# Kernel generation of a two-layer SSM and attention kernel: float32 identity matmuls for eight squarings and the coefficient sums

## Chip, cores, metric

The kernel runs on one core of one Trainium2 chip. The metric is device time in microseconds (us) of one execution, as the median of several runs. Engines are named as in the profile: PE (matrix engine; PEld its weight loads), DVE (vector engine), ACT (scalar engine), POOL (GpSimd), SP (the queue that issues nearly all DMAs).

## The reference

Four blocks work on x of shape 1 x 2048 x 512 in turn: dilated local attention (A), a state-space convolution (B), A, B. Both B blocks use the same parameters and so the same convolution kernel K, which depends on no activation:

```python
dt = jnp.exp(log_dt)[:, None]
logdA = dt * (A_re + 1j * A_im)
dB = dt * (B_re + 1j * B_im)
P = jnp.exp(logdA[:, :, None] * l[None, None, :])      # l = 0 .. 2047
K = jnp.einsum("dn,dnl,dn->dl", Cc, P, dB).real        # 512 x 2048
...
y = irfft(rfft(up) * rfft(Kp))[:L] + u * Dskip
x = x + A(layernorm(x)); x = x + B(layernorm(x)); x = x + A(layernorm(x)); x = x + B(layernorm(x))
```

Parameters and x are bfloat16.

## The kernel before

The program runs in stages: generation of K together with the start of the first attention layer (about 0 to 108 us), then the rest of attention, the convolution by a Fourier transform, and the two layers again. The change lies in the first stage, the function `k_gen`.

**How K is made.** With z = exp(dt * A), one complex number for each of 512 channels and 128 states, K at position l needs z to the power l. `k_gen` holds z as real and imaginary parts of 128 x 512 float32 (partition: state; free: channel) and squares it again and again: z, z^2, z^4, up to z^2048, eleven squarings k = 0 to 10. Before, one squaring was three instructions: `square(k)` on ACT squares both parts at once into `ws` (L1078), `double(k)` on DVE writes the imaginary part 2 * re * im (L1082), `differ(k)` on DVE writes the real part as the difference of the two squares (L1085). `power(k)` on ACT rounds each power to bfloat16 into one of two tables' seeds (L1096 into `Pw`, printed as `pow_t`, for k = 3 to 7; L1098 into `Bt`, printed as `B_t`, for the others), `power_neg(k)` stores the negated imaginary part (L1102 on ACT, L1104 on DVE).

**The coefficients.** `c_part` makes the complex product of B and dt * C: two float32 products into `t1` and `t2` (printed `t`), and their difference or sum into `c0` (printed `c_t`), all on DVE, all recorded at L1110, as `tt` is the helper there. Inputs arrive transposed by bfloat16 matmuls with `ident` or with the diagonal of dt (L1031) from `raw_*` tiles into PSUM tiles `pt`, a pool of four banks.

**The tables.** `bmul` fills `B_t` with products of powers (DVE, L1110; the temporary is `cm_t`). `table_head` (L1227) starts a chunk's table `A_t` with `c_t`; `levels` (DVE, L1110) doubles it five times with `pow_t`, two multiplies and an add per level. Four chunks of 32 channels use two buffers in turn. `product` (PE, L1268) multiplies `A_t` with `B_t` into `pk`, `produced` (ACT, L1276) copies that to `kgs`, from where DMAs store K.

**The other work of the stage.** Layer norm of x in four blocks: row sums on ACT (L1154, L145), means and variances on DVE (L1168, L1169, L1180), application on ACT and DVE (L195, L197), transposes on PE (L1196) and their evictions on ACT (L1199); projections on PE (L1206) and evictions on ACT (L1211). The stage ends with the first logits products `A_pr` on DVE (L342).

**The order.** Nothing is scheduled automatically here. `ORDERK` is a string that is walked letter by letter; each letter takes the next operation of one stream: s `square`, i `double` and `differ` in turn, b `power` and `power_neg`, C `c_part`, M `bmul`, T and U the levels of even and odd chunks, H a table head, l a, W, y, z, 3 the layer norm, t and e transposes and evictions, k q K Q projections and evictions, p and x products and evictions, c small DMAs, d loads of x, G and w constants and their store, o E copies within `kT_ext`, X the first logits products. Each engine runs its instructions strictly in the order in which the walk issued them, and waits on semaphores where it reads what another engine writes.

POOL makes constants in the first 15 us (`build_a_consts` and others): `ident`, `nident` (minus the identity), index tables and masks, all in bfloat16 or integers; `slot_mask` (L128) is the last of them.

Of the kernel before, what the change touches and what calls it, by code (L numbers as in the profile page):

```python
# [20 lines left out]
P = 128  # L21
# [13 lines left out]
N = 128  # L35
# [8 lines left out]
DQT = 8  # L44
NQT = DQG // DQT
ORDERK = """
isCbCiCbsiMaiCCbsiMiGGsbcCbMaTMiiMisMbiMbsGbMiGbiMTbcsibTTaiTcbTsbMTiiGbTGGsTMGciaiMTGMcabMGMaTM
asaMMGMlalTiWMlaaiyTbayiyTMawaMytatMTelkaeMsqMkdliqMaMKMaMMqMqWMlbQQMMMqMyHykUUakpKkyyttkaxUUpKU
kaUUUUaqUUxeUQppqHkdxxKUqeQTkTaUTklqT3paTqlKWTkQTplqkyqx3Ty3QKxT3TTpqlkTpyyHqWEUxktQlKtkUzkekeTK
zUUUkkzkUztKkKtkkTUpexUUKUEkUkeUkUKpKUokxkpxpKUkUxxkqUKEpxoqkkUpUUxopXXXKQpZxxZZ  # L50
"""
ORDER0 = """
KD KA KA KA KD KA KD KA KD KA KD kA KA kD KA KD UA KD UA UA UD KA kA kD kA UD
UA UD UA kD kA kD u UD u u UA m m m UA u u UD u UA m kD UA kD UA m
m u UA u m kA u kD u m kD u kD kA kA yA m YA m yD u yA u m m m
u u yA m m u YA m yA w000D yD yA YD yA w010D YA yD yA
"""
LATE0 = "a s t g r b m"
ORDERF = """
yA h00 YA h01 v100A v110D h10 a0 z12A p0 z11A n0D h11 w001A w011A S a1 p1 T0 E01A z13A E00D n1G H2  # L60
P02 a2 P00 Q00 p2 T1 E10D E11D P01 P11 P12 n2D H3 a3 P13 T2 P10 E20D E21D P03 p3 P21 P22 n3D
P23 T3 E30D E31A P20 x1
"""
ORDER1 = """
UA UD UA UD UA UA UD UA UD UD u u m m u u m m UA u UA UD m UA u u
UD UA u m m u u m m u YD m u YA YA m u yD m yA u u m m u w001A
m m yA yA w000D YA yD yA YD w011D yA yD w010D yA yD yA v101A v103D v113A v102D v112D v111D v110A v100A
"""

CORE0 = """  # L70
# [914 lines left out]
NIA = 32  # L985
CH = 32
NROW = 641


def k_gen(tc, nc, a_consts, ins, kd, la, x_v, lnst, zero, b_consts):  # L990

    B_L = (0, 1, 2, 3, 4, 5, 6, 7, 256, 258, 260, 262, 512, 516, 768, 772, 1024, 1280, 1536, 1792, 2048)
    NCH = P // CH
    with ExitStack() as ctx:
        pw = ctx.enter_context(tc.tile_pool(name="kg_pow", bufs=1))
        Bt = pw.tile([P, 2, P, NB, 4], BF16, name="B_t")
        Pw = pw.tile([P, NCH, 5, 4, 4 * CH], BF16, name="pow_t")
        c0 = pw.tile([P, 2, 4 * P], BF16, name="c_t")
        tab = [ctx.enter_context(tc.tile_pool(name="kg_tab0", bufs=1))]
        c_psum, c_small = ExitStack(), ExitStack()  # L1000
        sp = c_small.enter_context(tc.tile_pool(name="kg_small", bufs=1))
        pst = c_psum.enter_context(tc.tile_pool(name="kg_ps_t", bufs=4, space=PSUM))
        late = {}
        iotas, a_rest = a_consts(sp)
        ident = la.c["ident"]
# [13 lines left out]
        raw = {}  # L1019
        for name in ("A_im", "A_re", "B_re", "B_im", "C_re", "C_im"):  # L1020
            raw[name] = sp.tile([P, 4, N], BF16, name="raw_" + name)
            nc.sync.dma_start(raw[name][:], ins[name].rearrange("(t p) n -> p t n", p=P))
        x_load(0)
        zero()
        x_load(1)
# [22 lines left out]
        keyed()  # L1048
        steps, w2_store = rest()
        a_rest()  # L1050
        ws = sp.tile([P, 3, 4 * P], F32, name="ws")
        sn, cs = ws[:, 0], ws[:, 1]
        t1 = sp.tile([P, 4 * P], F32, name="t1")
        t2 = sp.tile([P, 4 * P], F32, name="t2")
        cur = {0: sp.tile([P, 2, 4 * P], F32, name="sq_z", tag="sq_z", bufs=2)}
        a_re, turn = cur[0][:, 0], ws[:, 2]
# [17 lines left out]
        nc.vector.tensor_tensor(cur[0][:, 1], a_re, sn, ALU.mult)  # L1074
        nc.vector.tensor_tensor(cur[0][:, 0], a_re, cs, ALU.mult)

        def square(k):
            nc.scalar.activation(ws[:, 0:2], cur[k][:], ACT.Square)  # L1078

        def double(k):  # L1080
            cur[k + 1] = sp.tile([P, 2, 4 * P], F32, name="sq_z", tag="sq_z", bufs=2)
            nc.vector.scalar_tensor_tensor(cur[k + 1][:, 1], cur[k][:, 0], 2.0, cur[k][:, 1], ALU.mult, ALU.mult)  # L1082

        def differ(k):
            nc.vector.tensor_tensor(cur[k + 1][:, 0], ws[:, 0], ws[:, 1], ALU.subtract)  # L1085

        def planes(k):
            return cur[k][:].rearrange("p r (c x) -> p r c x", c=NCH)

        def copy_by(eng):  # L1090
            return nc.scalar.copy if eng == "A" else nc.vector.tensor_copy

        def power(k):
            copy = copy_by(ENGK["b"][k + max(0, min(k - 3, 5))])
            if 3 <= k <= 7:
                copy(Pw[:, :, k - 3, 1::2, :].rearrange("p c r x -> p r c x"), planes(k))  # L1096
            else:
                copy(Bt[:, :, :, B_L.index(1 << k), :], cur[k][:].rearrange("p r (q g) -> p r q g", g=4))  # L1098

        def power_neg(k):  # L1100
            if ENGK["b"][2 * k - 2] == "A":
                nc.scalar.mul(Pw[:, :, k - 3, 2, :], planes(k)[:, 1], -1.0)  # L1102
            else:
                nc.vector.tensor_scalar(Pw[:, :, k - 3, 2, :], planes(k)[:, 1], -1.0, None, ALU.mult)  # L1104

        def power_copy(k):
            nc.sync.dma_start(Pw[:, :, k, 0, :], Pw[:, :, k, 1, :])
# [1 line left out]
        def tt(*args):  # L1109
            return lambda: nc.vector.tensor_tensor(*args)  # L1110

        def c_part():
            for q, (x0, y0, x1, y1, op) in enumerate((("C_re", "B_re", "C_im", "B_im", ALU.subtract),
                                                      ("C_re", "B_im", "C_im", "B_re", ALU.add))):
                yield tt(nat(t1[:]), T[x0], T[y0], ALU.mult)
                yield tt(nat(t2[:]), T[x1], T[y1], ALU.mult)
                yield tt(c0[:, q], t1[:], t2[:], op)

        def bmul(src, by, dst):
            s0, s1, st = src  # L1120
# [258 lines left out]
def kernel(  # L1379
# [200 lines left out]
```

## Time and profile before

| | us |
|---|---|
| median of 3 runs | 403.68 (402.94 to 405.08) |
| profiled execution, span from first to last instruction | 402.6 |
| DVE busy in the span | 383.5 |
| PE busy in the span | 328.0 |
| ACT busy in the span | 321.8 |
| POOL busy in the span | 59.1 |
| start of the first logits product on DVE (L342) | 103.41 |
| 11 squares on ACT (L1078), 128x1024 float32 | 1.05 each |
| 11 doublings (L1082) and 11 differences (L1085) on DVE | 0.68 each |
| 2 sums into c_t on DVE (L1110) | 0.73 each |

The profile is of one execution, so its span is compared with the runs' times only through the difference of 1.1 us to their median. The page gives busy time of each engine and, in 40 slices of 10 us, the busy share in tenths. In the order of time of an engine, each line has start, length, engine, source line, operation, written tile, read tiles, shape, and in square brackets how long the engine stood idle before it and who ended that. An instruction on DVE or ACT can start a little before the one ahead has ended, so the distance of starts is shorter than the length.

### The profile page before, as it was taken

What the parts mean: (1) busy time and instruction counts of PE and PEld (TensorE: products, weight loads), DVE (VectorE), ACT (ScalarE), POOL (GpSimd) and SP (SyncE); (2) the same over time, 40 slices, a digit from 0 to 9 for tenths busy, and PEclk for the clock granted to TensorE, in tenths of its full rate; (3) what the DMA queues carried; (4) which work ended last, traced back from release to release, by engine and by line L of the source; (5) the groups of instructions that cost most, each with busy time, mean ns of one, the idle gap of its engine ahead of it and who ended that gap; (6) DMA issues with size and microseconds to landing.
All of it is one profiled execution on the core that took longest, in us unless ns stands there. A gap on an engine that the chain in (4) does not pass through costs nothing.

```text
span 402.6 us, 14781 instructions
## 1 busy us (share of the span) xinstructions
PE 328.0 (81%) x6527; PEld 230.3 (57%) x6527; DVE 383.5 (95%) x460; ACT 321.8 (80%) x557; POOL 59.1 (15%) x75
## 2 busy tenths in 40 slices
PE   3000059999999989999998889999999998997895
PEld 2000026657735656756987888543456666566885
DVE  6999999999999999999999998979899999989994
ACT  7999888898656578988999987674666677989974
POOL 9402400000199500200600000100000001000000
PEclk9999997999999999999999999999999999999999
DMA  7952711115013875259236685730063019504606
GB/s 219 395 143 37 81 52 50 44 27 117 3 43 76 214 210 160 55 173 384 93 112 232 228 285 166 280 114 2 0 170 94 3 39 383 161 2 134 186 14 202
DMA packets 62323, 54.17 MB, mean 135 GB/s; under 512 B 33869, under 2 KB 50738, under 8 KB 60978
## 3 DMA queue, kind: packets, MB, share of 16 engines
q1 hardware_dynamic: 62250, 53.22, 43.5%
q8 instruction: 51, 0.84, 0.9%
q14 instruction: 14, 0.11, 0.1%
q10 hardware_dynamic: 8, 0.00, 0.0%
HBM read 30.15 MB, written 13.24 MB: 108 GB/s over the span
## 4 chain that ended last, share of the span: by engine, by line
PE 36%; DVE 31%; ACT 17%; issue 8%; DMA 5%; SPq 2%; POOL 1%; DVEq 0%; ACTq 0%; POOLq 0%
DVE pav L467 11%; PE pq L398 6%; PE pk L1268 5%; ACT a1s L791 5%; PE pp L1206 4%; DVE t L847 3%; PE pq L223 3%; DVE prod L342 3%; PE pp L282 3%; PE L L350 2%; ACT ub L860 2%; DVE B_t L1110 2%; DVE sq_z L1085 2%; DMA v_ext<-v_ext 2%; DMA kf_ring<-kf_dram 2%
## 5 line engine op out<-in xcount | busy, mean ns | idle before, releaser
L467 DVE TENSOR_TENSOR pav<-attn,v_ext 128x4096 bf16<-128x4096 bf16 (+1 forms) x34 | 72.4, 2168 | 0.4 <-DMA v_ext<-v_ext 0.3
L342 DVE TENSOR_TENSOR prod<-qT,kT_ext 128x4096 bf16<-128x4096 bf16 x29 | 67.0, 2341 | 1.4 <-PE L L350 0.9
L1196 PE MATMUL pt<-ident,x_blk 128*128 128x128 bf16 x64 | 5.9, 241 | 42.8 <-DVE x_blk L197 38.6
L1110 DVE TENSOR_TENSOR A_t<-A_t,pow_t 128x1024 bf16<-128x1024 bf16 (+4 forms) x46 | 38.3, 870 | 0.3
L492 PEld LDWEIGHTS <-pav 64*128 64x128 bf16 x1664 | 26.2, 95 | 13.5 <-DVE pav L467 8.6
L503 PE MATMUL pq<-wop,oT 128*128 128x512 bf16 x128 | 32.9, 379 | 0.7 <-ACT oT L494 0.7
L860 ACT CAST ub<-pb 128x1024 bf16<-128x1024 f32 x32 | 32.1, 1079 | 1.2 <-PE pb L809 1.2
L492 PE MATMUL po<-ident,pav 64*128 64x64 bf16 x1664 | 29.3, 190 | 4.2 <-DVE pav L467 3.2
L400 ACT CAST v_ext<-pq 128x512 bf16<-128x512 f32 x32 | 18.8, 586 | 16.2 <-PE pq L398 16.2
L809 PE MATMUL pb<-a1s,w_sb 128*128 128x64 bf16 x768 | 27.4, 193 | 5.0 <-ACT a1s L791 1.7
L398 PE MATMUL pq<-wv,xnT 128*128 128x512 bf16 x128 | 30.6, 380 | 0.0
L1206 PE MATMUL pp<-xnT,kT_ext 128*128 128x512 bf16 x96 | 27.1, 411 | 4.3 <-ACT kT_ext L1211 2.3
L1196 PEld LDWEIGHTS <-x_blk 128*128 128x128 bf16 x64 | 4.6, 107 | 44.8 <-DVE x_blk L197 38.8
L809 PEld LDWEIGHTS <-w_sb 128*128 128x128 bf16 x768 | 24.9, 98 | 7.2 <-issue 5.2
L791 ACT CAST a1s<-pb 128x1024 bf16<-128x1024 f32 x29 | 28.2, 1059 | 0.8 <-PE pb L802 0.8
L1268 PEld LDWEIGHTS <-A_t 128*64 128x64 bf16 (+1 forms) x512 | 22.9, 107 | 4.5 <-DVE B_t L1110 0.3
L1268 PE MATMUL pk<-B_t,A_t 128*64 128x84 bf16 (+1 forms) x512 | 24.6, 206 | 0.0
L791 DVE CAST a1s<-pb 128x1024 bf16<-128x1024 f32 x19 | 22.6, 1217 | 1.4 <-PE pb L802 1.3
L223 PE MATMUL pq<-xnT,kT_ext 128*128 128x512 bf16 x96 | 23.9, 380 | 0.0
L225 ACT CAST qT<-pq 128x512 bf16<-128x512 f32 x24 | 14.1, 586 | 9.3 <-PE pq L223 9.2
L509 ACT ACTIVATE x_sb<-pq 128x512 bf16<-128x512 f32 x24 | 14.3, 594 | 8.7 <-PE pq L503 8.7
L398 PEld LDWEIGHTS <-xnT 128*128 128x128 bf16 x128 | 11.6, 98 | 15.3 <-issue 3.0
(259 smaller groups left out, 897.0 us busy)
## 6 DMA issues: line engine op xcount, KB each, us to landing
w_sb<-w_dram SPq DMA_DIRECT2D x8, 1024.0 KB, 7.8
w_dram<-xnT SPq DMA_DIRECT2D x1, 4096.0 KB
kf_ring<-kf_dram SPq DMA_DIRECT2D x13, 256.0 KB, 4.8
kf_ring<-kf_dram SPq DMA_DIRECT2D x26, 128.0 KB, 4.3
v_ext<-v_ext SPq DMA_DIRECT2D x4, 784.0 KB, 6.6
x_blk<-in_A_x_dram SPq DMA_DIRECT2D x4, 512.0 KB, 4.1
kT_ext<-in_A_wqkv_dram SPq DMA_DIRECT2D x4, 512.0 KB, 9.2
x_sb<-in_A_x_dram SPq DMA_DIRECT2D x4, 512.0 KB, 5.3
```

Of the source, the lines that this page charges most:

```text
L223: nc.tensor.matmul(pq[:], lhsT=self.wqk[:, dt, ft * P:(ft + 1) * P], rhs=self.xnT[:, dt, q * 512:(q + 1) * 512], start=(dt == 0), stop=(dt ...
L342: nc.vector.tensor_tensor(pr, self.qT[q][:, ft].unsqueeze(1).to_broadcast([P, W, 4, P]), kap, ALU.mult)
L398: nc.tensor.matmul(pp[:], lhsT=xnT[:, dt, a * P:(a + 1) * P], rhs=wv[:, dt, :], start=(dt == 0), stop=(dt == NDT - 1))
L467: nc.vector.tensor_tensor(pv[:, i], attn[:, n % 4].unsqueeze(2).to_broadcast([P, W, DH // parts, H]), vap, ALU.mult)
L492: nc.tensor.matmul(po[:, h, 0, i * nt + ft, :], lhsT=pvf[rows, i, w, ft * P:(ft + 1) * P], rhs=ident[rows, rows], start=(w == 0 and ft + i ...
L503: nc.tensor.matmul(pw[:], lhsT=oT[:, ftp, :], rhs=self.wo[:, ftp, :], start=False, stop=(ftp == NDT - 1))
L791: (self.nc.scalar.copy if eng == "act" else self.nc.vector.tensor_copy)(dst, src)
L809: nc.tensor.matmul(p2[:, j, :], lhsT=self.w2[:, ec * EC + j, :], rhs=a1s[:, ec * EC + j, :], start=True, stop=True)
L860: nc.scalar.copy(ub[:], p2)
L1110: return lambda: nc.vector.tensor_tensor(*args)
L1206: nc.tensor.matmul(pps[kind, b, ft][:], lhsT=la.wqk[:, dt, c:c + P], rhs=la.xnT[:, dt, b * 512:(b + 1) * 512], start=(dt == 0), stop=(dt = ...
L1268: nc.tensor.matmul(o, lhsT=lhs, rhs=Bt[:, ri, c * CH + ql].rearrange("p b g -> p (b g)"), start=(not half and j % 4 == 0 and ri == 0), sto ...
```

## The change

The real part of a squaring is now made on PE for k = 3 to 10 (`SQ_PE = 3`): the identity times the first square plus the negated identity times the second, accumulated in one PSUM bank, in float32. The real part then stays in PSUM and is read there by `double`, `square` and `power`; the imaginary part has a tile of its own. Because the parts lie in different memories, `square` and `power` take two instructions of 512 where they took one of 1024. The two coefficient sums are made in the same way, with an ACT copy into `c_t`. POOL makes the float32 identities by two copies behind its other constants. Space comes from the raw tiles moving into the not yet used `qT` tiles and from a second pair of products placed in a not yet used part of `kT_ext`. `ORDERK` is another string of the same letters with the same counts. In the built program DVE has ten instructions fewer, ACT seventeen more (seven squares, eight power copies, two copies of sums), PE twenty float32 matmuls more, POOL two copies more; the number of DMAs is the same.

```diff
 ORDERK = """
-isCbCiCbsiMaiCCbsiMiGGsbcCbMaTMiiMisMbiMbsGbMiGbiMTbcsibTTaiTcbTsbMTiiGbTGGsTMGciaiMTGMcabMGMaTM
...
+isbCCiisisibsCCbCiiisCMMMbiTGsbbbMMMMMiiMMsbbiicTTTccasbGTTbTiiTTTcsiTTTGGiGGGbbbsGGMMMciiMaGMbaaa
...
+        ident32 = sp.tile([P, P], F32, name="ident32")
+        nident32 = sp.tile([P, P], F32, name="nident32")
+        nc.gpsimd.tensor_copy(ident32[:], ident[:])
+        nc.gpsimd.tensor_copy(nident32[:], la.c["nident"][:])
...
         def square(k):
-            nc.scalar.activation(ws[:, 0:2], cur[k][:], ACT.Square)
+            if k <= SQ_PE:
+                nc.scalar.activation(ws[:, 0:2], (im[k] or z0)[:], ACT.Square)
+                return
+            for r in range(2):
+                nc.scalar.activation(ws[:, r], cur[k][r], ACT.Square)
...
         def differ(k):
-            nc.vector.tensor_tensor(cur[k + 1][:, 0], ws[:, 0], ws[:, 1], ALU.subtract)
+            if k < SQ_PE:
+                cur[k + 1] = im[k + 1][:, 0], im[k + 1][:, 1]
+                nc.vector.tensor_tensor(cur[k + 1][0], ws[:, 0], ws[:, 1], ALU.subtract)
+                return
+            re = pst.tile([P, 4 * P], F32, name="pt")
+            nc.tensor.matmul(re[:], lhsT=ident32[:], rhs=ws[:, 0], start=True, stop=False)
+            nc.tensor.matmul(re[:], lhsT=nident32[:], rhs=ws[:, 1], start=False, stop=True)
+            cur[k + 1] = re[:], im[k + 1][:, 0]
...
+            for r, z in enumerate(cur[k]):
+                if 3 <= k <= 7:
+                    copy(Pw[:, :, k - 3, 1 + 2 * r, :], z.rearrange("p (c x) -> p c x", c=NCH))
+                else:
+                    copy(Bt[:, r, :, B_L.index(1 << k), :], z.rearrange("p (q g) -> p q g", g=4))
...
+        def c_sum(q, t):
+            pc = pst.tile([P, 4 * P], F32, name="pt")
+            nc.tensor.matmul(pc[:], lhsT=ident32[:], rhs=t[0], start=True, stop=False)
+            nc.tensor.matmul(pc[:], lhsT=(ident32 if q else nident32)[:], rhs=t[1], start=False, stop=True)
+            nc.scalar.copy(c0[:, q], pc[:])
+
+        prods = [(t1[:], t2[:]), [la.kT[:, 3, a:a + 8, :].rearrange("p a q -> p (a q)").bitcast(F32) for a in (14, 22)]]
...
-                yield tt(c0[:, q], t1[:], t2[:], op)
+                yield tt(nat(t[0]), T[x0], T[y0], ALU.mult)
+                yield tt(nat(t[1]), T[x1], T[y1], ALU.mult)
+                yield lambda: c_sum(q, t)
```

More of the change, by code (lines that the diff above doesn't have):

```diff
@@ L46 @@
 ORDERK = """
-isCbCiCbsiMaiCCbsiMiGGsbcCbMaTMiiMisMbiMbsGbMiGbiMTbcsibTTaiTcbTsbMTiiGbTGGsTMGciaiMTGMcabMGMaTM
-asaMMGMlalTiWMlaaiyTbayiyTMawaMytatMTelkaeMsqMkdliqMaMKMaMMqMqWMlbQQMMMqMyHykUUakpKkyyttkaxUUpKU
-kaUUUUaqUUxeUQppqHkdxxKUqeQTkTaUTklqT3paTqlKWTkQTplqkyqx3Ty3QKxT3TTpqlkTpyyHqWEUxktQlKtkUzkekeTK
-zUUUkkzkUztKkKtkkTUpexUUKUEkUkeUkUKpKUokxkpxpKUkUxxkqUKEpxoqkkUpUUxopXXXKQpZxxZZ
+isbCCiisibsCCbCiiisCMMMbiTGsbbbMMMMMiiMMsbbiicTTTccasbGTTbTiiTTTcsiTTTGGiGGGbbbsGGMMMciiMaGMbaaa
+aaisiMTMGMMlaaawMMlWMbaMsMMlMMiiyMTaaaMMMayylyaMlMbWMMMttHeeqlkkUUUUyqppyyyttUQUUdKqxxaaqakQpapk
+akkUKUUdkHUUxkUKKx3a3qTTUTqqeTTqppeQTTTTQx3TaaqqqqQpllQTWxqqlykk3QkkpTyTTKKyHUUkkUUkyKUUtxtkpeex
+lWkkUUKKlzzzEpkkzkkKxUUUUKttkUeUeUkpUKxkxkkkKKEEppUUooUUkkkkxxKKpoxXXqqQppXxxZZZ
 """
 ORDER0 = """
[L53 to L56, printed above, removed]
+KD KA KA KA KD KA KD KA KD KA KD kA KA kD KA KD UA KD UA UA UD KA kA kD kA UD UA UD UA kD kA kD u UD
+u u UA m m m UA u u UD u UA m kD UA kD UA m m u UA u m kA u kD u m kD u kD kA kA yA m YA m yD u yA u
+m m m u u yA m m u YA m yA w000D yD yA YD yA w010D YA yD yA
 """
@@ L60 @@
 yA h00 YA h01 v100A v110D h10 a0 z12A p0 z11A n0D h11 w001A w011A S a1 p1 T0 E01A z13A E00D n1G H2
-P02 a2 P00 Q00 p2 T1 E10D E11D P01 P11 P12 n2D H3 a3 P13 T2 P10 E20D E21D P03 p3 P21 P22 n3D
-P23 T3 E30D E31A P20 x1
+P02 a2 P00 Q00 p2 T1 E10D E11D P01 P11 P12 n2D H3 a3 P13 T2 P10 E20D E21D P03 p3 P21 P22 n3D P23 T3
+E30D E31A P20 x1
 """
 ORDER1 = """
-UA UD UA UD UA UA UD UA UD UD u u m m u u m m UA u UA UD m UA u u
-UD UA u m m u u m m u YD m u YA YA m u yD m yA u u m m u w001A
-m m yA yA w000D YA yD yA YD w011D yA yD w010D yA yD yA v101A v103D v113A v102D v112D v111D v110A v100A
+UA UD UA UD UA UA UD UA UD UD u u m m u u m m UA u UA UD m UA u u UD UA u m m u u m m u YD m u YA YA
+m u yD m yA u u m m u w001A m m yA yA w000D YA yD yA YD w011D yA yD w010D yA yD yA v101A v103D v113A
+v102D v112D v111D v110A v100A
 """
@@ L987 @@
 NROW = 641
+SQ_PE = 3
 def k_gen(tc, nc, a_consts, ins, kd, la, x_v, lnst, zero, b_consts):
@@ L1019, in k_gen @@
         raw = {}
+        q0, q1 = (la.qT[b][:].rearrange("p t a q -> p (t a q)") for b in range(2))
         for name in ("A_im", "A_re", "B_re", "B_im", "C_re", "C_im"):
-            raw[name] = sp.tile([P, 4, N], BF16, name="raw_" + name)
-            nc.sync.dma_start(raw[name][:], ins[name].rearrange("(t p) n -> p t n", p=P))
+            home = (q0, q1)[len(raw) // 4]
+            raw[name] = home[:, len(raw) % 4 * 512:(len(raw) % 4 + 1) * 512].rearrange("p (t n) -> p t n", n=N)
+            nc.sync.dma_start(raw[name], ins[name].rearrange("(t p) n -> p t n", p=P))
         x_load(0)
@@ L1054, in k_gen @@
         t2 = sp.tile([P, 4 * P], F32, name="t2")
-        cur = {0: sp.tile([P, 2, 4 * P], F32, name="sq_z", tag="sq_z", bufs=2)}
-        a_re, turn = cur[0][:, 0], ws[:, 2]
+        z0 = sp.tile([P, 2, 4 * P], F32, name="sq_z", tag="sq_zFalse", bufs=2)
+        cur = {0: (z0[:, 0], z0[:, 1])}
+        a_re, turn = cur[0][0], ws[:, 2]
         p_im = turned_by("A_im", by_dt)
@@ L1073, in k_gen @@
             T[name] = nat(b[:])
-        nc.vector.tensor_tensor(cur[0][:, 1], a_re, sn, ALU.mult)
-        nc.vector.tensor_tensor(cur[0][:, 0], a_re, cs, ALU.mult)
+        nc.vector.tensor_tensor(cur[0][1], a_re, sn, ALU.mult)
+        nc.vector.tensor_tensor(cur[0][0], a_re, cs, ALU.mult)
+        im = {0: None}
         def square(k):
-            nc.scalar.activation(ws[:, 0:2], cur[k][:], ACT.Square)
+            if k <= SQ_PE:
[3 more added lines that the diff above has]
+                nc.scalar.activation(ws[:, r], cur[k][r], ACT.Square)
         def double(k):
-            cur[k + 1] = sp.tile([P, 2, 4 * P], F32, name="sq_z", tag="sq_z", bufs=2)
-            nc.vector.scalar_tensor_tensor(cur[k + 1][:, 1], cur[k][:, 0], 2.0, cur[k][:, 1], ALU.mult, ALU.mult)
+            z = sp.tile([P, 1 if k >= SQ_PE else 2, 4 * P], F32, name="sq_z", tag=f"sq_z{k >= SQ_PE}", bufs=2)
+            nc.vector.scalar_tensor_tensor(z[:, 0 if k >= SQ_PE else 1], cur[k][0], 2.0, cur[k][1], ALU.mult, ALU.mult)
+            im[k + 1] = z
         def differ(k):
-            nc.vector.tensor_tensor(cur[k + 1][:, 0], ws[:, 0], ws[:, 1], ALU.subtract)
-        def planes(k):
-            return cur[k][:].rearrange("p r (c x) -> p r c x", c=NCH)
+            if k < SQ_PE:
[6 more added lines that the diff above has]
+            cur[k + 1] = re[:], im[k + 1][:, 0]
         def copy_by(eng):
@@ L1094, in power @@
             copy = copy_by(ENGK["b"][k + max(0, min(k - 3, 5))])
[L1095 to L1098, printed above, removed]
+            if k <= SQ_PE:
+                z = (im[k] or z0)[:]
+                if k >= 3:
+                    copy(Pw[:, :, k - 3, 1::2, :].rearrange("p c r x -> p r c x"), z.rearrange("p r (c x) -> p r c x", c=NCH))
+                else:
+                    copy(Bt[:, :, :, B_L.index(1 << k), :], z.rearrange("p r (q g) -> p r q g", g=4))
+                return
+            for r, z in enumerate(cur[k]):
+                if 3 <= k <= 7:
+                    copy(Pw[:, :, k - 3, 1 + 2 * r, :], z.rearrange("p (c x) -> p c x", c=NCH))
+                else:
+                    copy(Bt[:, r, :, B_L.index(1 << k), :], z.rearrange("p (q g) -> p q g", g=4))
         def power_neg(k):
             if ENGK["b"][2 * k - 2] == "A":
-                nc.scalar.mul(Pw[:, :, k - 3, 2, :], planes(k)[:, 1], -1.0)
+                nc.scalar.mul(Pw[:, :, k - 3, 2, :], cur[k][1].rearrange("p (c x) -> p c x", c=NCH), -1.0)
             else:
-                nc.vector.tensor_scalar(Pw[:, :, k - 3, 2, :], planes(k)[:, 1], -1.0, None, ALU.mult)
+                nc.vector.tensor_scalar(Pw[:, :, k - 3, 2, :], cur[k][1].rearrange("p (c x) -> p c x", c=NCH), -1.0, None, ALU.mult)
         def power_copy(k):
@@ L1110, in tt @@
             return lambda: nc.vector.tensor_tensor(*args)
-        def c_part():
[L1113 to L1116, printed above, removed]
-                yield tt(c0[:, q], t1[:], t2[:], op)
+        def c_sum(q, t):
[4 more added lines that the diff above has]
+        prods = [(t1[:], t2[:]), [la.kT[:, 3, a:a + 8, :].rearrange("p a q -> p (a q)").bitcast(F32) for a in (14, 22)]]
+        def c_part():
+            for q, (x0, y0, x1, y1) in enumerate((("C_re", "B_re", "C_im", "B_im"), ("C_re", "B_im", "C_im", "B_re"))):
+                t = prods[q]
+                yield tt(nat(t[0]), T[x0], T[y0], ALU.mult)
+                yield tt(nat(t[1]), T[x1], T[y1], ALU.mult)
+                yield lambda: c_sum(q, t)
         def bmul(src, by, dst):
```

## The prediction

> **What bounds the kernel now.** I read the page first (busy time, slices), then the table by stretches of time, then the order of time of each engine for the first 110 us, because the change touches kernel generation alone.
>
> ```profile
> PE 328.0 (81%) x6527; PEld 230.3 (57%) x6527; DVE 383.5 (95%) x460; ACT 321.8 (80%) x557; POOL 59.1 (15%) x75
> ...
> PE   3000059999999989999998889999999998997895
> ...
> DVE  6999999999999999999999998979899999989994
> ACT  7999888898656578988999987674666677989974
> ```
>
> ```profile
> 0.00:60.00 60.00, 9.75 (x53) 5.64 (x54) 55.97 (x100) 53.22 (x99) 20.22 (x46) 0.99 0.59 155
> 60.00:103.40 43.40, 41.27 (x540) 28.39 (x540) 42.13 (x68) 37.83 (x70) 0.00 (x0) 0.93 0.24 56
> ```
>
> The columns of the second fence are length, then PE, PEld, DVE, ACT and POOL busy, granted clock, DMA share, GB/s. In the first 60 us DVE is busy 55.97, ACT 53.22, PE 9.75: two full engines and an empty one. From 60 to 103.4 (where the first logits product starts on DVE) DVE and PE are both full. So time taken from DVE in the first 60 us is worth its full length if neither ACT nor a new wait takes it back; ACT has only 6.8 us of room.
>
> ```profile
> 11.00 0.68 DVE L1085 TENSOR_TENSOR sq_z<-ws 128x512 f32<-128x512 f32 x1
> 11.60 0.77 DVE L1110 TENSOR_TENSOR c_t<-t,t 128x512 bf16<-128x512 f32 x1
> 12.30 0.73 DVE L1082 SCALAR_TENSOR_TENSOR sq_z<-sq_z 128x512 f32<-128x512 f32 x1
> ...
> 17.36 0.69 DVE L1110 TENSOR_TENSOR c_t<-t,t 128x512 bf16<-128x512 f32 x1
> ...
> 18.30 0.23 DVE L1227 COPY A_t<-c_t 128x256 bf16<-128x256 bf16 x1
> ```
>
> The first two columns are start and length. A float32 row of 512 is listed with 0.68 us, but the next one starts 0.60 us later; I charge 0.60.
>
> **DVE's part.** Ten rows leave DVE: eight of the eleven L1085 subtractions (k = 3 to 10) and both c_t sums of L1110. 10 x 0.60 = 6.0 us. The doubling (L1082) stays and reads one operand in PSUM; the products at 9.81 do that and also stand 0.60 apart, so nothing is added.
>
> **The C sums, a new wait.** Each becomes two float32 matmuls and an ACT copy. The matmuls need the float32 identities, which POOL makes last.
>
> ```profile
> 9.31 1.11 POOL L114 TENSOR_SCALAR nident<-iota_id 128x128 bf16<-128x128 int32 x1
> ...
> 14.06 0.52 POOL L128 TENSOR_SCALAR slot_mask<-iota_slot_mask 4x16 bf16<-4x16 int32 x1
> ```
>
> POOL's list ends at 14.58; two 128x128 copies follow, each between 0.20 (the memset of that size at 1.03) and 1.11 (nident). With 0.5 the first sum cannot start before 15.1, although its products are ready at 11.1. No float32 matmul is in the trace. Below, one cannot be cheaper than one bf16 matmul of 512 columns; its price depends on the clock:
>
> ```profile
> 54.41 0.15 PEld L1206 LDWEIGHTS <-kT_ext 128*128 128x128 bf16 x1 [0.28 <-issue]
> 54.83 0.15 PEld L1206 LDWEIGHTS <-kT_ext 128*128 128x128 bf16 x1 [0.28 <-issue]
> ...
> 116.54 2.76 PE L398 MATMUL pq<-wv,xnT 128*128 128x512 bf16 x12
> 119.14 0.59 PE L425 MATMUL L<-mx,nident 128*128 128x512 bf16 x2
> ```
>
> After a pause the matmuls between these weight loads follow each other at 0.43 us; in the steady stretch it is (119.14 - 116.54) / 12 = 0.22. Above, a product of two float32 numbers cut into three bf16 parts each would be nine such passes. DVE's rows charge a float32 operand twice a bf16 one (0.60 for 512 against 0.60 for 1024 at 41.43), so I take two parts per operand, 2 x 2 = 4 passes: 1.72 us at half clock, 0.87 at full. [...]
>
> PE has been idle since 8.4, so the first sum runs at half clock: 15.1 + 2 x 1.72 + 0.2 of drain = 18.7. Its copy (L1141) stands on ACT behind the square of k = 2 and ahead of the B_t copy of k = 2, the square of k = 3 and the second copy, so ACT stands still from 14.6 to 18.7, then does copy 0.5, B_t copy 0.95 and square 0.95 to 21.1; the second sum is ready about 21.2 (half of it at full clock), copied by 21.8. DVE's table head (18.30 above) reads both and stands in the new order after one doubling more and two sums less: due at 18.2, it waits 3.6 us, with all of DVE's queue behind it. The ends: 0.9 with one pass, 9 with nine. A wait of 0.5 for the square of k = 1 is added at 12.3, where the c_t sum used to stand.
>
> **The squarings.** One round from k = 3 on: square of the real part 0.6 (512 on ACT), two matmuls 1.73 at full clock, drain and handovers 0.3: 2.6 us. In the trace the squares of k = 4 to 8 start at 20.87, 23.28, 27.26, 30.29 and 33.64, 3.2 apart, so at full clock the rounds lie beside DVE's other work and cost nothing. Uncovered, at half clock, a round is 0.6 + 3.44 + 0.3 = 4.3, 1.1 late each, and DVE's next doubling with all behind it waits. Which clock?
>
> ```profile
> 52.44:55.85 3.41, 3.16 (x15) 1.00 0.40 107
> 55.85:59.26 3.41, 1.40 (x8) 1.00 0.12 47
> 59.26:62.68 3.42, 2.29 (x7) 0.50 0.00 0
> 219.69:223.10 3.41, 2.22 (x66) 1.00 0.81 299
> ```
>
> Columns: length, PE busy, clock. A stretch with 3.16 of 3.41 busy was followed by full clock, one with 1.40 by half, 2.29 did not lift it again; 2.22 at 219.69 did not drop it. The sums and the first squaring keep PE full from 15.1 to about 22, so it goes to full clock there; then 1.73 of every 2.8 to 3.0 is 60%, which kept it. The last two or three squarings lie 5 to 7 us apart (25 to 35% busy) and fall back to half. [...]
>
> **ACT.** Seven squares and eight power copies become two halves (2 x 0.50 for 0.95, +0.05 to 0.1 each, 15 times: 1.0), two C copies add 1.0. With the standstill (4.1, and 0.1 before the second copy) ACT is 6.2 later, less some 3.8 us of idle time it has from 25 to 60: about 2.4 late at 60. Its rows there feed the transposes and B_t. PE waited 3.1 us between 56.6 and 61 for ACT's evictions in the old order, so nothing covers it in PE. The late half-clock squarings lie here too. Ends 0 and 2.8; I take 1.4.
>
> **Order written anew.** The table's rows now stand as multiply, multiply, add directly behind one another. A dependent neighbour costs 0.11 more (27.87 to 28.18 is 0.31, an independent one 0.20); about nine more of them up to the first logits: 1.0. Moved DMAs: the same 251 on SP's queue in nearly the same order; the raw loads get another home (qT, first written at 60.34), and so does the second pair of products (columns of kT_ext, first written at 57.98), both long after their last reader. POOL's two copies are followed by nothing before 38. After 60 us the order of the chunks is shuffled with the same rows; nothing is charged, with 1 us either way.
>
> **Sum:** -6.0 + 0.5 + 3.6 + 1.4 + 1.0 = +0.5 us. Profiled span 402.6 becomes 403.1; the runs shown have a median 1.1 above that span (403.68), so 404.2. What this kernel can tell from no change is about 0.5%, 2.0 us.
>
> **Rivals.**
>
> 1. *Cheap float32 matmuls, faster.* With two passes (0.86 at half clock) the first sum is out at 17.0, the second copy done at 19.8: DVE waits 1.6; rounds are 1.8, late ones harmless, ACT 0.5 late. -6.0 + 0.5 + 1.6 + 0.5 + 0 to 0.5 = -3.4 to -2.9: 400.5. For it: only one operand carries more than bf16 (the identity is 0, 1, -1). Against it: the identity was widened to float32, so the operation is float32 in both.
>
> 2. *PE stays at half clock through the squarings, slower.* Place: the doublings of k = 4 to 8. Each round 4.3 for 3.2, five rounds late by 1.1 = 5.5, stall at the table head 4.2. -6.0 + 0.5 + 4.2 + 5.5 + 1.4 + 1.0 = +6.6: 410.3. It decides once a round exceeds the 2.8 to 3.2 us that DVE's rows give it, that is once a float32 matmul takes more than some 1.1 us. For it: 2.29 of 3.41 busy did not lift the clock at 59.26, and rounds are lighter than that. Also for it: a weight load of its own in each pass (0.1, the page's PEld L1196 has a mean of 107 ns) left uncovered would bring 0.87 to 1.27. Against it: PE is solidly busy from 15.1 to 22. If it were both, or nine passes, the eighth squaring would reach past 55 and push the transposes behind it on PE; that goes beyond 415.
>
> 3. *The saving arrives whole.* If the sums hid wholly (identities early, full clock) -6.0 + 0.5 + 1.0 + 0 = -4.5: 399.2. POOL's end at 14.58 speaks against it.
>
> **How the numbers follow.** The even case has 0.47 (own range 401.5 to 407), rival 1 with rival 3 0.25, rival 2 with its worse forms 0.28. Of the even case 0.03 lies below 401.7 and 0.07 above 405.7. So faster 0.28, same 0.37, slower 0.35. The range takes in rival 1 and most of rival 2: 400.2 to 411.
>
> **What would show it.** Right: ACT idle some 4 us before the first c_t copy, released by PE; DVE idle 3 to 4 us before COPY A_t<-c_t; float32 rows of about 1.7 us at 15 us and 0.9 later; DVE ten rows fewer; the first logits product (L342 at 103.41) within 2 us of where it was. Wrong: rows of about 0.5 (rival 1), or sq_z doublings waiting on PE 1 us each from 25 to 45 (rival 2). A granted clock other than half at 15 us would undo the stall's size.

## The result and the profile after

The changed kernel takes 405.04 us (median of 20 runs, 404.1 to 407.14), the kernel before 404.06 (20 runs beside them). The ratio is 1.0026, interval 1.0015 to 1.0038: 1.0 us slower, which is clear of the noise but within the bound of 0.5% that the prediction takes as no change, and 0.8 us from the 404.2 predicted. The profiled span is 403.9 (402.6 before).

From the page of the changed kernel, and from its table by stretches (length, then PE, PEld, DVE, ACT, POOL busy, clock, DMA share, GB/s):

```profile
PE 345.7 (86%) x6519; PEld 238.4 (59%) x6567; DVE 378.1 (94%) x450; ACT 324.1 (80%) x574; POOL 54.2 (13%) x77
```

```profile
0.00:60.00 60.00, 29.82 (x81) 12.57 (x82) 53.01 (x94) 53.20 (x111) 15.46 (x48) 0.88 0.57 148
60.00:103.40 43.40, 41.84 (x541) 29.23 (x550) 40.10 (x65) 39.79 (x76) 0.00 (x0) 0.93 0.27 66
```

DVE has ten instructions and 5.4 us of work less. PE has 17.7 us more. ACT is as full in the first 60 us as it was (53.20; 53.22 before). In order of time, the places that the prediction named, on POOL, PE and ACT:

```profile
13.66 0.28 POOL L1055 CAST ident<-ident 128x128 f32<-128x128 bf16 x1
13.90 0.28 POOL L1056 CAST nident<-nident 128x128 f32<-128x128 bf16 x1
```

```profile
13.99 2.07 PE L1139 MATMUL pt<-t,ident 128*128 128x512 f32 x2 [5.77 <-POOL ident L1055]
15.86 1.91 PE L1140 MATMUL pt<-t,nident 128*128 128x512 f32 x2
17.57 1.32 PE L1139 MATMUL pt<-kT_ext,ident 128*128 128x512 f32 x2
18.73 1.02 PE L1140 MATMUL pt<-kT_ext,ident 128*128 128x512 f32 x2
20.34 1.13 PE L1103 MATMUL pt<-ws,ident 128*128 128x512 f32 x2 [0.60 <-ACT ws L1087]
...
44.91 2.08 PE L1103 MATMUL pt<-ws,ident 128*128 128x512 f32 x2 [6.00 <-ACT ws L1090]
```

```profile
17.81 0.59 ACT L1141 CAST c_t<-pt 128x512 bf16<-128x512 f32 x1 [3.15 <-PE pt L1140]
```

The first sum waits for POOL; from the start of its second matmul to the next sum is 17.57 - 15.86 = 1.71 us at half clock, and 0.97 at full between the two matmuls of a squaring (21.31 after 20.34). That the clock is half at 14 us is read from these lengths; the profile's clock column doesn't show it, as it reads 1.00 from 14.75 to 18.17. ACT stands still 3.15 us. DVE, four of its places:

```profile
20.80 0.25 DVE L1260 COPY A_t<-c_t 128x256 bf16<-128x256 bf16 x1 [2.44 <-ACT c_t L1141]
...
72.87 1.29 DVE L137 BATCH_NORM_STATS2 ln_bn<-x_blk 128x6 f32<-128x512 bf16 x2 [2.46 <-DMA x_blk<-in_A_x_dram]
...
103.36 6.69 DVE L341 TENSOR_TENSOR A_pr<-qT,kT_ext 128x4096 bf16<-128x4096 bf16 x3
...
116.08 1.23 DVE L413 TENSOR_REDUCE mx<-L 128x128 bf16<-128x1024 f32 x1 [1.25 <-PE L L324]
```

The table head waits 2.44. At 60.28 DVE starts the table of chunk 1, 2.7 us ahead of the kernel before (62.97). At 72.87 it has waited 2.46 for a load. The first logits product stands at 103.36 (103.41 before). The row `mx` at 116.08 is DVE's first maximum over the logits and is taken as the end of the stage from here on; it has waited 1.25 for PE, where the kernel before started it with no wait:

```profile
115.59 1.21 DVE L414 TENSOR_REDUCE mx<-L 128x128 bf16<-128x1024 f32 x1
```

So 0.5 of the 1.3 us by which the profiled spans differ lie in the stage, and 0.8 behind it. There PE stands still once near the end, and the trace shows nothing that released it:

```profile
394.59 0.19 PE L877 MATMUL pb<-WpJ,t 64*128 64x64 bf16 x1 [0.81 <-issue]
```

The profiles of e1 and e2 have it at the same row (0.76 and 0.52), that of the kernel before doesn't. It is most likely the greater part of the 0.8; its cause is open.

What PE did up to the end of the stage, first the kernel before, then the changed one (first projection and last table products):

```profile
53.60 2.98 PE L1206 MATMUL pp<-xnT,kT_ext 128*128 128x512 bf16 x8 [0.25 <-ACT xnT L1199]
...
104.89 4.34 PE L1268 MATMUL pk<-B_t,A_t 128*128 128x84 bf16 x96
```

```profile
60.40 0.59 PE L1239 MATMUL pp<-xnT,kT_ext 128*128 128x512 bf16 x1 [1.80 <-ACT xnT L1232]
...
107.20 2.91 PE L1301 MATMUL pk<-B_t,A_t 128*128 128x84 bf16 x64
```

PE starts its projections 6.8 us later and ends its table products at 110.1 instead of 109.2, almost without a pause in between. So three theories for why a lighter DVE brought nothing: LOAD (the wait at 72.87 took the lead back), HEAD (the late identities cost ACT, DVE and then PE), PE (PE's full stretch from 60 to 110 sets the end, and starts late).

### The profile page after: what moved, and what is told of

It is laid out like the page before. It is cut to its first block, busy times and chain, and to the rows that moved or that the text cites. A ratio compares the mean times of both kernels' runs of the same rounds, so it can differ in the third digit from the quotient of the medians.

```text
span 403.9 us, 14829 instructions
## 1 busy us (share of the span) xinstructions
PE 345.7 (86%) x6519; PEld 238.4 (59%) x6567; DVE 378.1 (94%) x450; ACT 324.1 (80%) x574; POOL 54.2 (13%) x77
## 3 DMA queue, kind: packets, MB, share of 16 engines
q1 hardware_dynamic: 62250, 53.22, 43.0%
## 4 chain that ended last, share of the span: by engine, by line
PE 37%; DVE 26%; ACT 18%; issue 6%; SPq 5%; DMA 4%; POOL 3%; DVEq 0%; ACTq 0%; POOLq 0%
DVE pav L466 7%; PE pq L397 6%; DVE A_t L1135 4%; PE pq L222 3%; PE pk L1301 3%; DVE t L846 3%; PE pp L281 3%; SPq L1406 3%; PE pp L1239 2%; PE pb L808 2%; ACT ln_junk L144 2%; PE L L349 2%; ACT ub L859 2%; ACT a1s L790 2%; DVE prod L341 2%
## 5 line engine op out<-in xcount | busy, mean ns | idle before, releaser
L502 PE MATMUL pq<-wop,oT 128*128 128x512 bf16 x123 | 31.9, 379 | 3.8 <-issue 2.5
L1239 PE MATMUL pp<-xnT,kT_ext 128*128 128x512 bf16 x87 | 23.8, 400 | 3.0 <-ACT xnT L1232 1.8
L1103 PE MATMUL pt<-ws,ident 128*128 128x512 f32 x16 | 10.2, 720 | 16.1 <-ACT ws L1090 15.5
L502 PEld LDWEIGHTS <-oT 128*128 128x128 bf16 x128 | 12.4, 98 | 13.4 <-ACT oT L493 1.3
```

Of the source, the lines that this page charges most:

```text
L502: nc.tensor.matmul(pw[:], lhsT=oT[:, ftp, :], rhs=self.wo[:, ftp, :], start=False, stop=(ftp == NDT - 1))
L1239: nc.tensor.matmul(pps[kind, b, ft][:], lhsT=la.wqk[:, dt, c:c + P], rhs=la.xnT[:, dt, b * 512:(b + 1) * 512], start=(dt == 0), stop=(dt = ...
```

## The experiments

All in one table, with 12 runs for each experiment (4 for e7 and e8). Ratio is to the kernel before on the same chip (403.85 to 404.18 in these comparisons). The last three columns are from the profiled execution: start of PE's first projection, end of its last table product, start of DVE's first `mx` (L413/L414), the end of the stage.

| run | median | ratio (interval) | first proj. | last product | mx |
|---|---|---|---|---|---|
| before | 404.06 | 1 | 53.60 | 109.23 | 115.59 |
| changed | 405.04 | 1.0026 (1.0015-1.0038) | 60.40 | 110.11 | 116.08 |
| e1 fill the DVE wait | 405.37 | 1.0030 (1.0006-1.0053) | 61.63 | 111.21 | 117.21 |
| e2 identities early | 402.06 | 0.9961 (0.9939-0.9983) | 57.97 | 106.94 | 112.93 |
| e3 fewer projections, changed | 402.92 | 0.9978 (0.9960-0.9996) | 60.40 | 108.57 | 114.55 |
| e4 fewer projections, before | 406.07 | 1.0040 (1.0019-1.0061) | 53.59 | 108.00 | 114.51 |
| e5 identities early, PE kept busy | 401.02 | 0.9921 (0.9894-0.9948) | 58.33 | 105.47 | 111.45 |
| e6 sums on DVE | 404.24 | 1.0016 (0.9988-1.0044) | 62.62 | 112.22 | 118.20 |
| e7 new code, old order | 415.80 | 1.0260 (1.0214-1.0306) | 66.38 | 120.18 | 127.29 |
| e8 old code, new order | 412.37 | 1.0204 (1.0165-1.0242) | 68.45 | 117.65 | 123.63 |
| e9 sums on DVE, PE warmed first | 403.67 | 1.0003 (0.9980-1.0026) | 59.63 | 108.34 | 114.31 |
| e10 changed, PE kept busy | 402.98 | 0.9979 (0.9961-0.9996) | 60.41 | 107.55 | 113.52 |
| e11 before, PE kept busy | 405.13 | 1.0031 (1.0015-1.0047) | 55.43 | 109.06 | 115.42 |
| e12 before, matmuls far ahead | 404.72 | 1.0017 (0.9998-1.0036) | 53.58 | 109.47 | 115.83 |

**e1: fill the wait for the load.** In `ORDERK`, one level step (U) of chunk 1 is taken ahead of the two statistics (3):

```diff
-akkUKUUdkHUUxkUKKx3a3qTTUTqqe...
+akkUKUUdkHUUxkUKKxU3a3qTTTqqe...
```

> The changed kernel with one multiply of the table's last level of chunk 1 (a DVE row of 2.29 us) moved ahead of the two row statistics of block 3, so that it lies in the 2.46 us that DVE waits for the load of block 3 at 70.4. Theory LOAD (that wait took back what DVE had gained): the first logits product comes from 103.36 to about 101.1 and the time falls by 2.3 us, to 402.7. Theory PE (PE is full from 60 to 110 and its last table product at 110.1 decides when DVE may go on at 116): the last product stays within 0.6 us, DVE's wait of 1.25 us at 116 grows by what DVE gains, the time stays within 0.6 us of 405.0.

DVE's order of time in e1:

```profile
69.22 4.49 DVE L1135 TENSOR_TENSOR A_t<-A_t,pow_t 128x4096 bf16<-128x4096 bf16 x2
73.93 1.29 DVE L137 BATCH_NORM_STATS2 ln_bn<-x_blk 128x6 f32<-128x512 bf16 x2 [0.21 <-DMA x_blk<-in_A_x_dram]
...
82.29 0.16 DVE L1201 SCALAR_TENSOR_TENSOR ln_msq<-ln_s 128x4 f32<-128x4 f32 x1 [1.01 <-ACT ln_junk L1187]
83.04 0.16 DVE L1202 SCALAR_TENSOR_TENSOR ln_veps<-ln_s,ln_msq 128x4 f32<-128x4 f32 x1 [0.59 <-ACT ln_junk L144]
```

The wait for the load went from 2.46 to 0.21, and nothing was gained: 1.0 and 0.6 us came back as waits for ACT's row sums, and the wait at `mx` grew from 1.25 to 1.55. From PE's first projection to its last table product it took 49.6 us here and 49.7 in the changed kernel. This profile has a handicap, as PE's first projection came 1.2 us late in it (see the last section); but the median of twelve runs shows no gain either, where LOAD asked for 2.3. LOAD falls; the stage follows PE. The wait for the load is itself PE's lateness: the queue that issues this load waits for PE's transposes,

```profile
SPq L1015 <- PE pt L1229: 15.1, 2, 9.7
```

(the changed kernel; us in total, times, longest), and where PE's transposes came earlier with DVE's order untouched (e5 and e10 below), DVE had no wait there.

**e2: the identities early.** POOL makes them behind the memset of `B_t`; the two copies at L1055 go.

```diff
+        ident32 = sp.tile([P, P], F32, name="ident32")
+        nident32 = sp.tile([P, P], F32, name="nident32")
+        nc.gpsimd.tensor_copy(ident32[:], ident[:])
+        nc.gpsimd.tensor_scalar(nident32[:], ident32[:], -1.0, None, ALU.mult)
         pdt = pst.tile([P, 4, P], F32, name="pt")
```

> The changed kernel with the two float32 identities made on POOL at about 4.8 us, ahead of its index tables and masks. Theory HEAD (the C sums wait for POOL from 11.1 to 14.0; ACT stands still 3.15 us there and DVE 2.44 at the table head; ACT is full until 60, so its delay goes on to the layer norm and to PE's first projection at 60.4): first sum at 11.2, ACT's 3.15 us and DVE's 2.44 us gone or under 0.6, first squaring on PE at about 17.5, first projection at about 57.5, last table product at about 107, time 2.5 to 3.3 us less, 402. Theory PE alone (PE's stretch starts late for another reason): DVE gains 2.4 us and gives them back at 70 and 116, time 404.5 to 405. Theory LOAD alone: DVE's wait at 70 grows from 2.46 to nearly 5 us, time 404 to 405.

PE and DVE of e2:

```profile
10.61 2.05 PE L1139 MATMUL pt<-t,ident 128*128 128x512 f32 x2 [3.19 <-POOL off_WpJ L662]
...
57.97 0.59 PE L1239 MATMUL pp<-xnT,kT_ext 128*128 128x512 bf16 x1 [1.80 <-ACT xnT L1232]
```

```profile
18.18 0.23 DVE L1260 COPY A_t<-c_t 128x256 bf16<-128x256 bf16 x1
```

The waits of 3.15 on ACT and 2.44 on DVE are gone, PE's first projection comes 2.4 us earlier, its last table product 3.2, and the time falls by 3.0 to 402.06, as HEAD said.

**e3 and e4: less work for PE.** In `proj`, in the changed kernel and in the one before:

```diff
-            for dt in range(2 * h, 2 * h + 2):
+            for dt in range(2 * h, 2 * h + 2) if kind == "k" else (3 * h,):
```

> The changed kernel without half of the contraction of the query projections (16 of 32 matmuls of 512 columns; the queries come out wrong). PE has 3.5 us less to do at full clock. Theory PE: the last table product comes 1.5 to 3 us earlier, DVE's wait of 1.25 us at 116 goes, time 1.3 to 3 us less, 402 to 403.7. Theory LOAD: only the two to four of these matmuls that stand ahead of the transposes at 67.6 count, the load comes 0.4 to 0.9 us earlier, time 0.4 to 0.9 us less.

> The kernel before without half of the contraction of the query projections (16 of 32 matmuls; the queries come out wrong). If DVE alone bounds the kernel before, as the prediction took it: no difference, within 0.4 us of 404.1, although PE has 3.5 us less to do. If PE bounds the stage there too: 1 us less or more.

In the changed kernel 3.5 us less work on PE bring 2.1 us: its last table product comes 1.5 earlier, the wait at `mx` is 0.47. PE holds. The rest of the 3.5 is not gained, since PE now waits 1.9 us for ACT's evictions of the queries. In the kernel before the stage also ends 1.1 us earlier, so DVE was not its only bound; yet the time is 2 us longer. In the profile 2.7 us are lost behind the stage. A standstill of PE at L492, for which the profile gives no releaser, is 1.0 us here and 0.3 in the kernel before. Why is open (e12).

**e5, e10, e11: PE kept busy.** Matmuls whose results nobody reads, in e5 and e10 (8 before the last squaring, 3 behind each of the first four transposes, 9 behind the block's last), in e11 with 15 between the projections instead of the first 8:

```diff
+            for _ in range(WARM.get(k, 0)):
+                nc.tensor.matmul(re[:], lhsT=ident[:], rhs=la.wqk[:, 0, 0:512], start=True, stop=True)
...
+                    n = WARM_T[a] if (b, d, di) == (0, 0, 0) else WARM_P if (b, d, di, a) == (0, 1, 1, 3) else 0
+                    if n:
+                        wu = pst.tile([P, 4 * P], F32, name="pt")
+                    for _ in range(n):
+                        nc.tensor.matmul(wu[:], lhsT=ident[:], rhs=la.wqk[:, 0, 0:512], start=True, stop=True)
```

> The kernel with early identities (402.1) and, beside it, 29 more bfloat16 matmuls on PE whose results nobody reads: 8 before the last squaring, 3 behind each of the first four transposes, 9 behind the last transpose of block 0. They are to keep PE busy from about 46 to 58, so that the projections from 58 on and the first table products run at full clock (in the early-identity profile the clock is half until 61.9). Theory CLOCK (PE sets the end of the stage, and its first 4 us there run at half clock): the six or seven projections from 58 take 1.5 us instead of 3.2, the last table product comes from 106.9 to about 105, time 1 to 2 us less, 400.1 to 401.1. Rivals: ACT's evictions, not PE, set the pace up to 65, then the time stays at 402 within 0.5; or the added matmuls stand in the way of transposes at half clock, then 1 us more.

> The changed kernel, its identities late as they are, with the 29 matmuls that nobody reads around the transposes of block 0 (as in the early-identity kernel that had them). Theory CLOCK: the first projections from 60.4 and table products from 63.8 at full clock, the last table product from 110.1 to about 108.5, time 1 to 1.5 us less than 405.0: 403.5 to 404. Rival (ACT's lateness alone sets it): 405 within 0.4.

> The kernel before with 36 matmuls that nobody reads around its transposes of block 0 and between its first projections, so that PE has full clock from about 54 on instead of half from 59.3 to 66.1. If DVE bounds the kernel before: 404.1 within 0.5. If PE's clock costs there what it costs in the changed kernel: the last table product 1 us earlier than 109.2 and 1 us less, 403.1.

PE of e5 (first projections, and the end):

```profile
58.33 1.94 PE L1249 MATMUL pp<-xnT,kT_ext 128*128 128x512 bf16 x8
60.11 2.91 PE L1311 MATMUL pk<-B_t,A_t 128*128 128x84 bf16 x64
...
102.56 2.91 PE L1311 MATMUL pk<-B_t,A_t 128*128 128x84 bf16 x64
```

Eight projections take 1.94 us, at full clock; in the changed kernel seven took 3.4 (60.40 to 63.77). PE's stretch shrinks from 49.0 in e2 to 47.1 us and the time by 1.0 to 401.02, faster than both kernels. Without the early identities (e10) the same matmuls bring 2.1 us, more than expected; PE's stretch is again 47.1. In the kernel before (e11) they give full clock as well (eight projections in 1.89 us from 55.43, against 2.98 from 53.60 in the kernel before, whose clock column reads 0.50 from 59.26 to 66.09), but the stage ends where it did (115.42 for 115.59). That fits DVE as the bound there: PE waits 1.1 us for a `B_t` row of DVE. It isn't a clean test, as the added matmuls also put the first projection 1.8 us later. The time is 1.1 us longer all the same, as neither theory had it; the profile has one standstill of PE behind the stage:

```profile
244.42 0.22 PE L874 MATMUL pb<-WpJ,t 128*128 128x128 bf16 x1 [1.75 <-issue]
```

**e6 and e9: the sums back on DVE; and with PE warmed ahead of the squarings.** e6, and in e9 beside it 24 matmuls before the first PE squaring:

```diff
-                yield lambda: c_sum(q, t)
+                yield tt(c0[:, q], t[0], t[1], ALU.add if q else ALU.subtract)
...
+            for _ in range(24 if k == SQ_PE else 0):
+                nc.tensor.matmul(re[:], lhsT=ident[:], rhs=warm_by[:], start=True, stop=True)
```

> The changed kernel with the two coefficient sums back on DVE (two rows of 0.6 us more there; no float32 matmul and no copy for them), the squarings still on PE. Theory HEAD: the waits for POOL's identities (ACT 3.15, DVE 2.44) and two ACT copies (1.0) go; the first projection on PE comes from 60.4 to about 57, the last table product from 110.1 to about 107.5, time 1.5 to 2.5 us less than 405.0: 402.5 to 403.5, nearly the early-identity kernel. Theory that the squarings on PE cost the time (half clock in the last ones, ACT's halves): no better than 404.5.

> The kernel with the sums on DVE (404.2) and, ahead of its first squaring on PE, 24 bfloat16 matmuls whose results nobody reads, from about 9.7 to 17.5, so that the squarings meet PE at full clock. Theory CLOCK (without the sums PE is cold; its first squarings run at half clock, 4.5 us apart instead of 2.7 to 3.2, and DVE waits 3.0, ACT 5.3 us for them): first squarings 2.7 to 3.2 apart, these waits of DVE under 0.5, PE's first projection from 62.6 to about 59, time 2 to 3 us less, 401.2 to 402.2. Rival (the sums on DVE cost 1.2 us and the order fits them badly, the clock is not the reason): 404 within 0.7.

The squarings on PE in e6, then in e9:

```profile
17.76 2.05 PE L1103 MATMUL pt<-ws,ident 128*128 128x512 f32 x2 [10.81 <-issue]
...
22.26 2.08 PE L1103 MATMUL pt<-ws,ident 128*128 128x512 f32 x2 [0.75 <-ACT ws L1090]
...
26.73 2.07 PE L1103 MATMUL pt<-ws,ident 128*128 128x512 f32 x2 [0.69 <-ACT ws L1090]
...
31.19 1.13 PE L1103 MATMUL pt<-ws,ident 128*128 128x512 f32 x2 [0.69 <-ACT ws L1090]
```

```profile
17.81 1.10 PE L1106 MATMUL pt<-ws,ident 128*128 128x512 f32 x2
...
20.51 1.12 PE L1106 MATMUL pt<-ws,ident 128*128 128x512 f32 x2 [0.75 <-ACT ws L1091]
...
23.56 1.12 PE L1106 MATMUL pt<-ws,ident 128*128 128x512 f32 x2 [1.07 <-ACT ws L1091]
```

Neither expectation of e6 held. Without the sums PE had rested for 11 us, the first three squarings ran at half clock, 4.5 us apart, and DVE waited 3.0 us for two doublings: this is rival 2 of the prediction, in a kernel where PE is cold. Warmed (e9), the same squarings follow at 2.7 to 3.6, the two DVE waits are gone, and PE's first projection comes 3.0 us earlier. The median moved by 0.6 only, which is inside the noise, not by the 2 to 3 expected. The runs of e6 lie in two groups (seven from 402.9 to 404.3, five from 406.7 to 407.3), and its profile is of a run of the upper one (407.24). That the cold start happens in only some executions would explain both, but this is not shown: no profile of the lower group was taken, and the mean granted clocks of the two groups overlap (0.959 to 0.974, and 0.966 to 0.975).

**e7 and e8: code and order apart.** The changed code walked by the old `ORDERK`, the old code by the new one.

> The changed code walked in the order of the kernel before. If the order matters little, as the prediction charged it (1 us for dependent neighbours, 1 us either way): 404 to 406. If the two belong together (in the old order the squares stand close ahead of the doublings that need them, and each PE squaring makes DVE wait 0.5 to 2.6 us): 409 to 413, with DVE waits at most of the doublings k = 4 to 10.

> The code before walked in the changed kernel's order. DVE has its ten rows more (6.0 us) and no wait at the table head. If the order matters little: 403.5 to 405.5. If the order costs by itself, since it puts the layer norm's transposes and PE's first projections behind the squarings: PE's first projection at 65 or later instead of 53.6, its last table product 5 us or more later than 109.2, time 408 to 412.

Neither works alone: 415.8 and 412.4, both a little beyond the dearer of their two expectations. DVE's longest waits, e7 first (columns: us in total, times, longest):

```profile
DVE B_t L1135 <- ACT B_t L1117: 6.7, 1, 6.7
DVE sq_z L1094 <- ACT ws L1090: 4.5, 3, 2.1
DVE A_t L1260 <- ACT c_t L1141: 2.6, 1, 2.6
DVE sq_z L1094 <- ACT pow_t L1121: 2.5, 1, 2.5
```

```profile
DVE sq_z L1085 <- ACT ws L1078: 3.6, 2, 3.3
```

In the old order DVE meets ACT's standstill for the identities at once (6.7, a `B_t` copy queued behind the `c_t` copy), and waits at four of the doublings. In the new order with the old code PE's first projection comes at 68.45 and its stretch ends at 117.65. The length of that stretch goes with the order, not with the code: 53.6 to 55.9 us in the old order (the kernel before, e4, e7, e11, e12), 47.1 to 49.7 in the new one (the changed kernel, e8 and all the others). The new order makes PE's dense part shorter and starts it later.

**e12: what happens behind the stage.** The kernel before, with 36 matmuls that nobody reads, which ran from 9.7 to 20.4 us:

```diff
+        wu = pst.tile([P, 4 * P], F32, name="pt")
+        for _ in range(36):
+            nc.tensor.matmul(wu[:], lhsT=ident[:], rhs=b[:], start=True, stop=True)
```

> The kernel before with 36 matmuls that nobody reads (as many as in the kernel before with matmuls around its transposes), all put into PE's idle time from about 10 to 25. They end 20 us before PE has anything else to do, so the first stage should be the kernel before's: first logits product at 103.4, last table product at 109.2. Theory POSITION (behind the first stage PE stands still at single places, 0.3 to 1.8 us, released by nothing that the profile shows; these places are the same in kernels with the same number of PE instructions ahead of them and differ where that number differs): the still-stand of about 1.8 us at the transform's matmuls near 245 comes back as in the kernel with 36 matmuls around the transposes, time 0.8 to 1.5 us more than before, 404.8 to 405.5. Rival (the added matmuls' place or the clock did it): nothing at 245, time 404 within 0.4.

The median of 404.72 lies between the two expectations, and its interval takes in no change. The standstill of 1.8 us at 245 did not come back; there is one of 0.5, elsewhere and later. POSITION isn't shown. The part behind `mx` (span less the start of `mx`) took 286.7 to 288.0 us in all these profiles except e4, with 289.7. What moves it is open.

## Why the prediction came out

It was right in the sum, and in part in its terms; that the sum was near zero was partly luck.

- *Ten DVE rows, -6.0, and the new order, +1.0.* Right. From 9.15 us to the first logits product, first the kernel before, then the changed one (length, DVE busy, rows, clock, DMA share, GB/s):

```profile
9.15:103.40 94.25, 92.69 (x149) 0.96 0.42 105
9.15:103.35 94.20, 87.68 (x139) 0.89 0.42 106
```

  Ten rows are gone and 5.0 us of busy time. With 6.0 for the ten, the others became 1.0 dearer; this is an estimate from the two lines. The saved 5.0 us turned into waits: the stretch is as long as it was.
- *Four passes per float32 matmul.* The time was right: 1.71 at half clock, where the rows of 0.43 gave 1.72. At full clock the first one behind a pause took 0.97 instead of 0.87. The count of four was the author's estimate from DVE's rows; the runs show the time alone. With two passes 0.86 was expected at half clock, so rival 1 is out.
- *Wait for the square of k = 1, +0.5.* 0.30.
- *Table head, +3.6.* The mechanism was right, the size too large: 2.44, and 3.15 instead of 4.1 on ACT. The mis-sized term is POOL: its list ended at 13.70 instead of 14.58, and the copies took 0.28 each instead of 0.5, so that the first sum began at 13.99 and not at 15.1. The 0.2 of drain is an estimate that no run shows by itself: ACT's first copy started 1.95 after the sum's second matmul (17.81 after 15.86), where 1.72 and 0.2 were charged.
- *Squarings free at full clock, the last ones at half.* Right: 2.7 to 3.2 us apart from 20.34 to 32.05, at half clock at 44.91 (2.08 us for its first matmul, 1.13 for that at 32.05). In the changed kernel rival 2 did not happen because the sums had warmed PE: the first matmul of the first squaring took 1.13 (20.34), against 2.05 in e6, where the sums are taken away, and 1.10 in e9, where 24 matmuls stand ahead of it. Uncovered at half clock, the rounds of e6 took 4.5, where 4.3 was charged; no run shows the 0.3 of drain and handovers in it by itself. In the two traces the profile's clock changes 3.41 us or multiples of it apart (in the kernel before at 59.26 and 66.09, in the changed one at 42.06, 48.89, 52.30 and 65.95). Rounds 60% busy kept the clock in the changed kernel's profile, as the prediction took it: it stayed full with 1.98 of 3.41 busy (28.41 to 31.82 us).
- *ACT, +1.4 at 60.* In the wrong place and too small. DVE waited for ACT nowhere between the table head and 60; PE's first projection came 6.8 us later. Part of that is ACT's standstill (e2 gave back 2.4). The rest is probably the new order, which puts more of the squarings ahead of the layer norm: with the old code (e8) it alone put the first projection at 68.45. No run separates it from ACT's additional copies.
- *"After 60 us the order of the chunks is shuffled ...; nothing is charged".* DVE's wait of 2.46 for a load lay there and was not seen. It follows from PE's lateness, and e1 shows that filling it gains nothing by itself. In DVE's sum it stands in for the 1.4 of ACT, and the head's 1.2 too much makes up for it: two errors that cancel.
- *DVE's queue alone was followed to the end of the stage.* This is the gap. The text saw PE full after 60 and then summed DVE's row only. In the changed kernel the last table product is PE's first projection plus 47 (full clock) to 50 us (its start at half clock), in e1, e2, e5, e6, e9 and e10 alike, and `mx` follows 6.0 us behind it in each of them. DVE's 2.7 us of lead at 60 were spent in waits. With both faults mended (e5) the lead reaches the end: 3.2 us less than the kernel before, by the medians of that comparison (401.02 and 404.18). So most of rival 3 was within reach, and the sum near zero was partly luck: a smaller head wait than charged, and a bound on PE that was not charged. Of the 1.3 us that the profiled spans differ, only 0.5 lie in this stage; the rest lies behind it, and PE's standstill of 0.81 at 394.59 there stays open.

## What to carry to other kernels

When an engine gives work to an idle one, look for the next engine that is full behind it: the saving counts only if that one can start earlier too (DVE led by 2.7 us at 60, and by 0.05 at the first logits product). Make what the new work needs (here two small constants) before its first use, since a full engine that waits early passes its delay on (3.0 us in e2). PE should be at full clock when a dense part of its work begins: matmuls that nobody reads brought 1.0 and 2.1 us here where PE set the end (e5, e10), and nothing in the kernel before (e11). A hand-written order belongs to the code that it was made for: each without the other was 8 to 12 us slower here.

## What the runs showed of the hardware

- A float32 matmul of 512 columns is listed as two rows. In the changed kernel their starts lie 0.85 us apart at half clock (15.01, 15.86) and 0.43 at full (20.88, 21.31); the weight loads of 0.19 to 0.33 us run beside them.
- PE's clock did not change at the same times in two executions of the same instructions. In e1, which has the changed kernel's up to 70 us, the sixth PE squaring ran at half clock, 2.07 us for its first matmul:

```profile
37.05 2.07 PE L1103 MATMUL pt<-ws,ident 128*128 128x512 f32 x2 [2.89 <-ACT ws L1090]
```

  In the changed kernel's profile it started at 36.93 and took 1.13. PE's first projection came 1.2 us later in e1's profile, most likely for this. Of a time with such a spread (404.1 to 407.1), one profile shows one case.
- PE can stand still for 0.5 to 1.8 us with no releaser in the trace, at places that differ between kernels with the same later instructions: 1.75 us at 244.42 in e11, 0.5 at 394.00 in e12, 0.81 at 394.59 in the changed kernel, none of them in the kernel before. The cause is open.
- POOL's small rows are not of one length: the same L668 took 0.18 us in the changed kernel and 0.68 in e2, and the row that makes `slot_sel` 0.96 in the kernel before and 0.52 in the changed one. The list's earlier end (13.70 for 14.58) comes from such rows.
